# Value products of two groups and the gate product of one as seven block products, on one core

## The chip, the core and the metric

The kernel runs on one core of one Trainium2 chip. A time is the device time in microseconds of one execution on that core. Before the change the median of three executions is 239.04 us (238.83 to 239.19).

## What is computed

Attention first, then a gated feed-forward block on its output:

```python
B, H, S, D = 4, 8, 768, 64                 # q, k, v: float32 (B, H, S, D)
scores = q @ k.transpose(0, 1, 3, 2) / sqrt(D)
# heads 0, 2 and 6: causal. All others: causal, and only the first 4 keys
# and the 64 newest ones
a = softmax(where(mask, scores, -1e9))
x = (a @ v).transpose(0, 2, 1, 3).reshape(3072, 512)

gate = x @ w_gate                          # w_gate, w_val: (512, 1536)
val = x @ w_val
out = (gate * sigmoid(gate) * val) @ w_out # w_out: (1536, 512), out: float32
```

## The kernel before

**Tiles and groups.** The 3072 tokens are 24 tiles of 128, in six groups (g = 0 to 5) of four tiles, 512 tokens each. The inner dimension of 1536 is cut into 12 slices of 128 (j = 0 to 11); NJ is 12 and NK is 6. Attention is done tile by tile (tasks sc, ex, mask, val, nm: scores on TensorE, exponential on ScalarE, mask on VectorE or GpSimd, value product on TensorE, norm on VectorE). The normed tile is transposed, for 16 of the 24 tiles by a DMA that SP issues (xdma), into xt, which holds a group's x with the model dimension on partitions: 128 x 4 blocks x 512 tokens, f16.

**The feed-forward block of a group.** For each slice j: four matmuls of a 128x128 block of w_gate against 512 columns of xt, summed in one PSUM bank (task gate{g}.{j}); four for w_val into another bank (vals{g}.{j}); a tanh on ScalarE that reads the gate bank and writes sig; on VectorE the first combine, (tanh + 1) * gate, which reads sig and the gate bank and writes sil (f32, SBUF); and the second combine, 0.5 * sil * val, which reads sil and the value bank and writes slice j of h (f16, SBUF). These are the lines L759 (matmuls of both), L765, L769 and L775. Group 0 does its first slices in halves of 256 columns.

**The output product.** h (512 tokens x 1536) times w_out (1536 x 512) is done per group as a product of 2x2 blocks with seven block products instead of eight (Strassen's scheme in Winograd's form). Sums of blocks of w_out are made once (L412). Sums of blocks of h (hs{g}.{x}.{part}, x = 1 to 4 in two parts each, L831) are made by VectorE or GpSimd, 128x768 f16 with both operands in SBUF. The products out{g}.p1 to p7 (L860, 12 matmuls of 256 columns each) go into banks, and ScalarE and VectorE gather them into the output tile (oe tasks; the adds are L898), which a DMA stores (st tasks). In group 5, p2 and p3 add into banks of p1 and p5, in two parts, and come last.

**What sets the order.** All tasks are listed once, with the engines that may do each, what it depends on and which buffers it takes. Three strings of digits then settle the rest: ORDER is one global order of all tasks and some filler matmuls (each engine's program follows it), WAYS picks the engine of each task, and SLOTS the buffer or PSUM bank. The program waits for what a task depends on and for the last user of its buffer; it makes no choice at run time. The rings of buffers are these, and a gate or value bank, an attention bank or an output bank is any of eight PSUM banks of 512 f32:

```python
RINGS = {"raw": 11, "hq": 5, "e": 6, "xb": 3, "xt": 2, "sig": 2, "sil": 3,
         "ps": 8, "gv": 8, "o": 8, "big": 8}
```

h_sb holds two groups (g % 2); the second combine of group g therefore also waits for output products and sums of group g - 2 that read the same slices (`was`). Loads of the weights go through raw tiles (128 x 1024 f32) and are cast to f16. Plain copies and casts go through one function, at L206 where ScalarE does them and at L208 where VectorE or GpSimd does.

Of the kernel before, what the change touches and what calls it, by code (L numbers as in the profile page):

```python
# [7 lines left out]
FP = mybir.dt.float32  # L8
# [8 lines left out]
    "06000307090A0401081U0D1V1cy11W1X0C1d1f1e0B2021021g280g1i2229231h2B2A1j0m1r2C0h1Y1p1s2D1a0F1Z2N1q"  # L17
    "2X1b1k2E0G2O1l2W1t1m2F1u2L1x1v1w2f2M1n2g2c1y1oxk2h0n27242d25262e2l2i2m2G1z0E0y2H2I2P0z2Q2j8e2R2t"
    "8o0k8f112o2x8p8g302p108q2U312J0i132V8h2K8r2y050H8t8s8y8i8u2k983C8w8v8m323D8j2n2z3I0q8k9D8x991493"
    "3J8l9A3L8z8n94380l91903K96950o2Z9E929B3M979G2Y9F0I3N9C3U339H1C3R3V2a2q2r0j342b9h2s3S162u3O3W9c9i"  # L20
    "0r3T3X9j359d363b9I3P0J3E372v9J3Q3f3i1D2w9N9e0K1F3A9O9f3B3g2S3H9k0p179P3G0v9m9g393F9l9Q9n3h0s3Y3j"
    "9K3Z0u199r3u3a3c3n9R0x3l9s401G3k3m0w9L3o0L3d9M9S3v419o9u2T9t0M9T3p429U433w3q9v441A9p3r450R4C493e"
    "1B469q4A9X4H3y3s4B9Y9a479Z9V3t4D9b3x4Q4N4K9W4OAu9z480O4LAQ9y1H18AnA00tB2Av124RAz1EAw0P4EB0A1BE4Z"
    "B1Ap4V4Y4gB34FBH4GBF0NAxAq1Q1K4hBGAV5CArAkAWBIB41IAl0QAX1J15AY4eAy1S4IB7AZAm0SALAR3z4JAoB51MAs4d"
    "AS9wAt4f1RAM5DANB91TB69x5KBCB8BA4b5fBBAa0WBD5I4o4i4l4P4pA2A45l4m1LA34M5FAT0U1N5E4S5L1PAUAf4jA5A8"
    "1OAg4v5JAbAh4a4k4TAcAE5g4UA95n4y514q4c4zAAA60V4r0a6KACAB5o5GA7AF4WAdAD524n4sAGAiAeAK540TAj505T55"
    "4t5mAO4u5U5MAP565W4x5753AHBM4wBLBJBN5NAI5c5VAJ58595XBO4XBR5A5H5O5BBK5v5p5sBP5wBX5q5Y0YBQ600Z5r5Z"
    "5t5a0XBV5b6I5u6366BWCb6E6HBS645iCe5h6N67BY5PBTCC6O5QBbCD5R7O5d6PCM6wCc6v5xCd0cBZ68CECN71BcCF6JBa"
# [91 lines left out]
def kernel(  # L120
# [837 lines left out]
    def tasks_of_sevens(g, T_h):  # L958
# [169 lines left out]
```

## Time and profile before

| what | value |
|---|---|
| median of 3 executions | 239.04 us (238.83 to 239.19) |
| profiled execution | 239.03 us |
| its span, first to last instruction | 237.2 us |
| PE (matmuls) busy | 230.5 us, 97% |
| PEld (weight loads) busy | 146.0 us, 62% |
| DVE (VectorE) busy | 194.5 us, 82% |
| ACT (ScalarE) busy | 141.2 us, 59% |
| POOL (GpSimd) busy | 110.6 us, 47% |
| granted TensorE clock | 1.000 |
| bytes moved by DMA | 40.73 MB |

The profiled execution lies within 0.01 us of the median, so its parts may be set against the median. Busy time is a share of the span; the 1.8 us between span and execution time lie before the first and behind the last instruction. A row of a group of instructions gives line, engine, operation, what it writes and reads, its shape and type and the count, then the busy time and the mean of one in ns, then the idle time of the engine just before them and what ended it. "banks" is PSUM; every other name (raw, e, sig, sil, h_sb, hs_sb, out_sb, xt, wg_sb) is in SBUF. A row of a timeline gives the start in us from the start of the span, the length in us, and then the instruction, with the idle time before it in brackets. In the 40 slices each digit is the busy share of a slice of 5.9 us in tenths.

### The profile page before, as it was taken

What the parts mean: (1) busy time and instruction counts of PE and PEld (TensorE: products, weight loads), DVE (VectorE), ACT (ScalarE), POOL (GpSimd) and SP (SyncE); (2) the same over time, 40 slices, a digit from 0 to 9 for tenths busy, and PEclk for the clock granted to TensorE, in tenths of its full rate; (3) what the DMA queues carried; (4) which work ended last, traced back from release to release, by engine and by line L of the source; (5) the groups of instructions that cost most, each with busy time, mean ns of one, the idle gap of its engine ahead of it and who ended that gap; (6) DMA issues with size and microseconds to landing.
All of it is one profiled execution on the core that took longest, in us unless ns stands there. A gap on an engine that the chain in (4) does not pass through costs nothing.

```text
span 237.2 us, 5639 instructions
## 1 busy us (share of the span) xinstructions
PE 230.5 (97%) x2211; PEld 146.0 (62%) x2211; DVE 194.5 (82%) x362; ACT 141.2 (59%) x217; POOL 110.6 (47%) x132
## 2 busy tenths in 40 slices
PE   7899999999999999999999999999999999999994
PEld 2577865655457778655464557766555565557883
DVE  2689999998999699698968989786969867788873
ACT  3699999889599879839575485384242232231010
POOL 7386577937484940998600550884000000525500
PEclk9999999999999999999999999999999999999999
DMA  6999999999999999999798124011620000220044
GB/s 173 351 343 366 326 346 356 358 350 296 271 238 165 236 291 182 289 164 188 196 171 207 34 48 87 4 22 20 203 44 0 3 0 0 87 92 1 20 183 155
DMA packets 67194, 40.73 MB, mean 172 GB/s; under 512 B 25184, under 2 KB 61024, under 8 KB 67168
## 3 DMA queue, kind: packets, MB, share of 16 engines
q1 hardware_dynamic: 65248, 37.50, 63.4%
q10 hardware_dynamic: 1920, 2.88, 3.3%
q8 instruction: 17, 0.28, 0.5%
q14 instruction: 9, 0.07, 0.1%
HBM read 28.31 MB, written 6.29 MB: 146 GB/s over the span
## 4 chain that ended last, share of the span: by engine, by line
PE 92%; DVE 3%; DMA 2%; ACT 1%; issue 0%; DVEq 0%
PE banks L759 51%; PE banks L860 23%; PE banks L567 8%; PE banks L597 6%; PE banks L473 2%; DMA raw<-in_q_dram 2%; PE banks L621 1%; DVE wt_sb L412 1%; DVE sil L769 1%; ACT hq L206 0%; PE banks L321 0%; DVE kT L208 0%; DVE hq L212 0%; DVE qT L208 0%; DVE xb L605 0%; DVE h_sb L775 0%
## 5 line engine op out<-in xcount | busy, mean ns | idle before, releaser
L765 ACT ACTIVATE sig<-banks 128x512 f32<-128x512 f32 (+1 forms) x76 | 42.7, 574 | 54.6 <-PE banks L759 47.5
L759 PE MATMUL banks<-xt,wg_sb 128*128 128x512 f16 (+1 forms) x304 | 71.4, 368 | 0.5 <-DVE sil L769 0.5
L759 PE MATMUL banks<-xt,wv_sb 128*128 128x512 f16 (+1 forms) x304 | 70.9, 368 | 0.0
L579 ACT ACTIVATE e<-banks 128x1024 f16<-128x1024 f32 (+2 forms) x68 | 59.5, 910 | 15.0 <-PE banks L567 6.3
L769 DVE SCALAR_TENSOR_TENSOR sil<-sig,banks 128x512 f32<-128x512 f32 (+1 forms) x76 | 48.8, 655 | 14.3 <-ACT sig L765 13.6
L775 DVE SCALAR_TENSOR_TENSOR h_sb<-sil,banks 128x512 f16<-128x512 f32 (+1 forms) x76 | 48.9, 655 | 2.8 <-PE banks L759 1.8
L860 PEld LDWEIGHTS <-h_sb 128*128 128x128 f16 x420 | 40.4, 98 | 8.5
L759 PEld LDWEIGHTS <-wv_sb 128*128 128x128 f16 x304 | 28.6, 98 | 26.9
L759 PEld LDWEIGHTS <-wg_sb 128*128 128x128 f16 x304 | 28.1, 98 | 27.2 <-issue 0.8
L587 POOL TENSOR_TENSOR e<-e,m 128x640 f16<-128x640 f16 (+1 forms) x17 | 28.0, 1655 | 19.8 <-ACT e L579 19.4
L831 POOL TENSOR_TENSOR h_sb<-h_sb 128x768 f16<-128x768 f16 x13 | 21.2, 1640 | 22.5 <-DVE hs_sb L831 16.7
L898 DVE TENSOR_TENSOR out_sb<-banks,out_sb 128x512 f32<-128x512 f32 x37 | 25.1, 688 | 7.4 <-PE banks L860 7.0
L860 PE MATMUL banks<-wt_sb,h_sb 128*128 128x256 f16 x216 | 26.2, 273 | 0.0
L831 POOL TENSOR_TENSOR hs_sb<-h_sb 128x768 f16<-128x768 f16 x3 | 4.9, 1639 | 45.1 <-PE banks L860 41.2
L860 PE MATMUL banks<-wo_sb,h_sb 128*128 128x256 f16 x204 | 25.1, 273 | 0.0
L597 PEld LDWEIGHTS <-e 128*128 128x128 f16 x472 | 18.0, 97 | 5.8 <-DVE e L587 0.2
L567 PEld LDWEIGHTS <-kT 64*128 64x128 f16 x472 | 14.4, 94 | 9.3 <-issue 8.7
L567 PE MATMUL banks<-qT,kT 64*128 64x128 f16 x472 | 19.7, 218 | 0.2 <-ACT qT L206 0.2
L597 PE MATMUL banks<-vt,e 128*128 128x65 f16 x472 | 19.7, 193 | 0.1
L206 ACT CAST hq<-raw 128x1024 f16<-128x1024 f32 (+1 forms) x16 | 14.7, 936 | 5.2 <-DMA raw<-in_q_dram 3.2
L605 DVE TENSOR_TENSOR xb<-banks,rc 128x512 f16<-128x512 f32 x24 | 16.6, 692 | 0.8
L208 POOL CAST vt<-raw 64x512 f16<-64x512 f32 x23 | 14.0, 607 | 2.3 <-DMA raw<-in_v_dram 1.3
(64 smaller groups left out, 192.9 us busy)
## 6 DMA issues: line engine op xcount, KB each, us to landing
raw<-in_v_dram SPq DMA_DIRECT2D x12, 512.0 KB, 5.8
raw<-in_q_dram SPq DMA_DIRECT2D x8, 512.0 KB, 6.2
raw<-in_k_dram SPq DMA_DIRECT2D x8, 512.0 KB, 5.3
raw<-in_moe_w_gate_dram SPq DMA_DIRECT2D x6, 512.0 KB, 8.6
raw<-in_moe_w_val_dram SPq DMA_DIRECT2D x6, 512.0 KB, 8.2
raw<-in_moe_w_out_dram SPq DMA_DIRECT2D x6, 512.0 KB, 7.9
out_dram<-out_sb SPq DMA_DIRECT2D x6, 512.0 KB, 4.4
raw<-in_q_dram SPq DMA_DIRECT2D x8, 256.0 KB, 6.4
```

The costliest lines, as they stand in the source:

```text
L567: nc.tensor.matmul(sc[:, c:c + n, :], weights, moving, start=first, stop=last)
L579: nc.scalar.activation(out=to, in_=src, func=AF.Exp, scale=scale)
L587: ENG[task().way].tensor_tensor(out=ev, in0=ev, in1=mm, op=ALU.mult)
L597: nc.tensor.matmul(avs[t][:, odd, n * 66:n * 66 + 65], ee, vv, start=(m == 0), stop=(m == len(bl) - 1))
L605: nc.vector.tensor_tensor(out=xb.rearrange("p n o d -> p o n d"), in0=av[:, :, :, 0:64], in1=rc.to_broadcast([128, 2, 4, 64]), op=ALU.mult)
L759: nc.tensor.matmul(ps, wsb[:, kk, j * 128:(j + 1) * 128], xt[:, kk, c[0]:c[1]], start=(kk == 0), stop=(kk == 3))
L765: nc.scalar.activation(out=sg[g, j, c], in_=gs[g, j, c], func=AF.Tanh, scale=0.5)
L769: nc.vector.scalar_tensor_tensor(out=sl[g, j, c], in0=sg.pop((g, j, c)), scalar=1.0, op0=ALU.add, in1=gs.pop((g, j, c)), op1=ALU.mult)
L775: nc.vector.scalar_tensor_tensor(out=hs[g, j][:, c[0]:c[1]], in0=sl.pop((g, j, c)), scalar=0.5, op0=ALU.mult, in1=vs.pop((g, j, c)), op1=A ...
L831: ENG[T_hs[g, x][part].way].tensor_tensor(out=to, in0=a, in1=b, op=op)
L860: nc.tensor.matmul(rooms[g, p][:, x, lo:hi], left[:, j, 128 * x:128 * x + 128], right[:, j, lo:hi], start=(on is None and (j == 0 if apart ...
L898: nc.vector.tensor_tensor(out=cell(*to), in0=room, in1=plus, op=ALU.add)
```

## The change

The value products of groups 4 and 5 and the gate product of group 5 are done as the output product is: x (512 tokens x 512) and the weight matrix (512 x 1536) are cut into 2x2 blocks, and seven block products replace eight. Three pairs s = 0, 1, 2 each hold slices 2s and 2s+1 of the lower half of j and 6+2s and 7+2s of the upper half.

- *Sums of the weights* (vw{i}.{kk}{mat}, i = 1 to 4, two parts; L1054): 16 subtractions of 128x768 f16, ten on GpSimd and six on VectorE. Those of w_val lie in raw tiles, those of w_gate in e and hq tiles.
- *Sums of x* (xs{g}.{i}; L1084): four of 128x512 f16 for each of the two groups, five on GpSimd and three on VectorE, in a raw tile.
- *Products* (wp{g}.{s}.{p}{mat}; L1104): four matmuls of 256 columns each. Products 1, 6, 7 and 4 add up in one bank X and the bank is copied after each; product 2 has bank Y; 5 and then 3 add up in bank Z.
- *Copies* (wy; 41 on ScalarE, 4 on VectorE, through the same copy function) of a bank of 128x512 f32 into half a raw tile: r1 after product 1, u2 after 6, u3 after 7, c21 after 4, y2 after 2.
- *Adds*: c11 = r1 + y2, both in SBUF (wa, nine: eight on GpSimd, one on VectorE); c22 = u3 + Z after product 5 and c12 = u2 + Z after product 3 (wb, 18, VectorE); all L1125.
- tanh and the combines then read the cells c11, c21, c12, c22 in SBUF where they read banks before. The new forms are tanh_w, stt1_w (L1142) and stt2_w (L1148).

Of 76 gate tasks 64 are left and of 76 value tasks 52; 63 products come. Of the sums of h, VectorE does 19 instead of 31 and GpSimd 29 instead of 17. All three strings are new throughout, so the whole program is ordered anew; the filler matmuls just ahead of the first gate are five instead of nine. Lines that were there before stand three further down (L206 is L209, L759 is L762, L831 is L834, L898 is L901).

```diff
+    WINO = {"v": (4, 5), "g": (5,)}
+    HJ = DFF // 2
...
+    def msum(mat, i, kk):
...
+        if i in (1, 3):
+            a, b = MB[mat, i // 2, 1][:, kk], MB[mat, 0, i // 2][:, kk]
+        else:
+            a, b = MB[mat, 1, 1 if i == 2 else 0][:, kk], m_sums[mat, i // 2, kk]
+        ENG[T_mw[mat, i][kk].way].tensor_tensor(
+            out=m_sums[mat, i, kk], in0=a, in1=b, op=ALU.subtract)
...
+    def xsum(g, i):
...
+        a, b, op = {1: (A[1, 0], A[1, 1], ALU.add), 2: (Z[:, 0], A[0, 0], ALU.subtract),
+                    3: (A[0, 0], A[1, 0], ALU.subtract),
+                    4: (A[0, 1], Z[:, 1], ALU.subtract)}[i]
+        ENG[T_xs[g, i].way].tensor_tensor(out=Z[:, i - 1], in0=a, in1=b, op=op)
+
+    W_ON = {1: "X", 6: "X", 7: "X", 4: "X", 2: "Y", 5: "Z", 3: "Z"}
+
+    def w_product(mat, g, s, p):
+        A = x_blocks(g)
+        left = {1: A[0, 0], 2: A[0, 1], 4: A[1, 1]}.get(p)
+        if left is None:
+            left = x_sums[g][:, {5: 0, 6: 1, 7: 2, 3: 3}[p]]
...
+        begins = p in (1, 2, 5)
+        if begins:
+            w_rooms[on] = buf("gv", [128, 2, 256], FP, "gv")
+        for m in range(2):
...
+            for kk in range(2):
...
+                nc.tensor.matmul(
+                    w_rooms[on][:, m], right, left[:, kk],
+                    start=(begins and m == 0 and kk == 0), stop=(kk == 1),
+                    skip_group_check=True)
...
+    def w_copy(mat, g, s, name):
+        to = w_cell(mat, g, s, name)
+        copy(T_wc[mat, g, s, name], to, w_rooms[mat, g, s, "Y" if name == "y2" else "X"])
+
+    def w_add(mat, g, s, name):
+        to = w_cell(mat, g, s, name)
+        other = w_cell(mat, g, s, "y2") if name == "c11" else w_rooms[mat, g, s, "Z"]
+        ENG[T_wc[mat, g, s, name].way].tensor_tensor(out=to, in0=other, in1=to, op=ALU.add)
...
+    def stt1_w(g, j):
+        c = (0, 512)
+        sl[g, j, c] = buf("sil", [128, 512], FP, "sil")
+        nc.vector.scalar_tensor_tensor(
+            out=by_halves(sl[g, j, c]), in0=by_halves(sg.pop((g, j, c))), scalar=1.0,
+            op0=ALU.add, in1=w_cells("g", g, j), op1=ALU.mult)
+
+    def stt2_w(g, j):
+        hs[g, j] = h_sb[:, g % 2, j]
+        nc.vector.scalar_tensor_tensor(
+            out=by_halves(hs[g, j]), in0=by_halves(sl.pop((g, j, (0, 512)))),
+            scalar=0.5, op0=ALU.mult, in1=w_cells("v", g, j), op1=ALU.mult)
...
+            p1 = product(1, xs + w_lo)
+            r1 = copied("r1", [p1])
+            p6 = product(6, [r1, T_xs[g, 2]] + T_mw[mat, 2])
+            u2 = copied("u2", [p6])
+            p7 = product(7, [u2, T_xs[g, 3]] + T_mw[mat, 3])
+            u3 = copied("u3", [p7])
+            p4 = product(4, [u3] + T_mw[mat, 4])
+            p2 = product(2, xs + w_lo)
+            y2 = copied("y2", [p2, r1])
...
+            c11 = added("c11", [y2])
+            c21 = copied("c21", [p4, c11])
...
+            p5 = product(5, [T_xs[g, 1]] + T_mw[mat, 1])
+            c22 = added("c22", [p5, u3])
+            p3 = product(3, [c22, T_xs[g, 4]] + w_hi)
+            c12 = added("c12", [p3])
```

Two places show how the instructions stand. The first is VectorE in group 5, where its gate and value slices are combined. Before:

```order
L831 TENSOR_TENSOR h_sb<-h_sb 128x3x256
L775 SCALAR_TENSOR_TENSOR h_sb<-sil,banks 128x512
L831 TENSOR_TENSOR h_sb<-hs_sb,h_sb 128x3x256
L769 SCALAR_TENSOR_TENSOR sil<-sig,banks 128x512
L831 TENSOR_TENSOR h_sb<-hs_sb,h_sb 128x3x256
L775 SCALAR_TENSOR_TENSOR h_sb<-sil,banks 128x512 x2
L769 SCALAR_TENSOR_TENSOR sil<-sig,banks 128x512
L775 SCALAR_TENSOR_TENSOR h_sb<-sil,banks 128x512
L898 TENSOR_TENSOR out_sb<-banks,out_sb 128x2x256
```

The same stretch of VectorE's program after the change:

```order
L1142 SCALAR_TENSOR_TENSOR sil<-sig,raw 128x512
L1125 TENSOR_TENSOR raw<-banks,raw 128x512
L1142 SCALAR_TENSOR_TENSOR sil<-sig,raw 128x512 x2
L1148 SCALAR_TENSOR_TENSOR h_sb<-sil,raw 128x512 x2
L1142 SCALAR_TENSOR_TENSOR sil<-sig,raw 128x512
L1148 SCALAR_TENSOR_TENSOR h_sb<-sil,raw 128x512 x2
L1125 TENSOR_TENSOR raw<-banks,raw 128x512 x2
L1142 SCALAR_TENSOR_TENSOR sil<-sig,raw 128x512 x2
L1125 TENSOR_TENSOR raw<-banks,raw 128x512 x2
L1148 SCALAR_TENSOR_TENSOR h_sb<-sil,raw 128x512
```

The combines read a raw tile where they read a bank; adds of cells from banks stand between them, and the sums of h (L831) have left this stretch for GpSimd.

The second place is GpSimd's program from its last masks to its last sum. Before, behind the masks:

```order
L587 TENSOR_TENSOR e<-e,m_103 128x640
L587 TENSOR_TENSOR e<-e,m_102 128x1024
L831 TENSOR_TENSOR h_sb<-h_sb 128x3x256
L831 TENSOR_TENSOR hs_sb<-h_sb 128x768 x2
L831 TENSOR_TENSOR h_sb<-h_sb 128x3x256 x3
L831 TENSOR_TENSOR hs_sb<-h_sb 128x768
L831 TENSOR_TENSOR h_sb<-h_sb 128x3x256
```

After the change a part of the list reads:

```order
L1125 TENSOR_TENSOR raw<-raw 128x512
L1054 TENSOR_TENSOR e<-wg_sb 128x768
L1084 TENSOR_TENSOR raw<-xt,raw 128x512
L1054 TENSOR_TENSOR e<-wg_sb 128x768
L1054 TENSOR_TENSOR e<-wg_sb,e 128x768
L1125 TENSOR_TENSOR raw<-raw 128x512
L1084 TENSOR_TENSOR raw<-xt 128x512 x2
L1054 TENSOR_TENSOR e<-wg_sb 128x768
L1084 TENSOR_TENSOR raw<-raw,xt 128x512
L1125 TENSOR_TENSOR raw<-raw 128x512
L834 TENSOR_TENSOR h_sb<-h_sb 128x3x256
L1054 TENSOR_TENSOR hq<-wg_sb,e 128x768
```

Where eight sums of h stood behind the last masks, sums of the weights and of x, adds of cells and 17 sums of h now stand, of which this is the part ahead of group 5's.

235 lines of the change are left out of this document (180 added, 55 removed).

## The prediction

> **What bounds the kernel now.** I read the first part of the page, then the slices, the chain that ended last, and the windows of the last third.
>
> ```profile
> PE 230.5 (97%) x2211; PEld 146.0 (62%) x2211; DVE 194.5 (82%) x362; ACT 141.2 (59%) x217; POOL 110.6 (47%) x132
> ...
> PE   7899999999999999999999999999999999999994
> ...
> DVE  2689999998999699698968989786969867788873
> ...
> POOL 7386577937484940998600550884000000525500
> ...
> PE 92%; DVE 3%; DMA 2%; ACT 1%; issue 0%; DVEq 0%
> ```
>
> TensorE is the bound: busy in every slice, 92% of the chain. VectorE is the second engine; GpSimd (POOL) idles for most of the last quarter.
>
> ```profile
> 170.00:200.00 30.00, 30.00 (x199) 17.39 (x196) 23.09 (x41) 8.19 (x15) 0.00 (x0) 1.00 0.08 24
> 200.00:234.00 34.00, 33.72 (x247) 23.85 (x244) 27.51 (x47) 6.06 (x11) 11.35 (x7) 1.00 0.22 80
> ```
>
> The columns are the length, then PE, PEld, DVE, ACT and POOL busy. From 170 us on PE never stops, and POOL runs seven instructions in all. What the change spends, it spends in this stretch.
>
> The one hole in PE's work after the start is worth a look, because the change multiplies its cause:
>
> ```profile
> 59.43 1.04 POOL L208 CAST hq<-raw 128x1024 f16<-128x1024 f32 x1 [1.46 <-DMA raw<-in_q_dram]
> ...
> 59.53 1.21 DVE L412 TENSOR_TENSOR wt_sb<-wo_sb 128x512 f16<-128x512 f16 x1
> ...
> 61.73 1.46 PE L759 MATMUL banks<-xt,wg_sb 128*128 128x512 f16 x6 [0.50 <-DVE sil L769]
> ...
> L412 DVE TENSOR_TENSOR wt_sb<-wo_sb x3: 411/414/1212, 59.5 to 62.8; 128x512 f16<-128x512 f16 x3
> ...
> L831 DVE TENSOR_TENSOR h_sb<-h_sb x9: 548/552/559, 87.7 to 220.6; 128x768 f16<-128x768 f16 x9
> L587 DVE TENSOR_TENSOR e<-e,m x21: 483/683/693, 23.7 to 169.0; 128x1024 f16<-128x1024 f16 x14, 128x640 f16<-128x640 f16 x7
> ...
> L769 DVE SCALAR_TENSOR_TENSOR sil<-sig,banks x76: 413/682/690, 21.0 to 218.4; 128x512 f32<-128x512 f32 x68, 128x256 f32<-128x256 f32 x8
> ...
> 39.34 0.69 DVE L587 TENSOR_TENSOR e<-e,m 128x1024 f16<-128x1024 f16 x1
> ...
> 39.76 1.16 POOL L208 CAST wg_sb<-raw 128x1024 f16<-128x1024 f32 x1 [1.18 <-DMA raw<-in_moe_w_gate_dram]
> ```
>
> A DVE subtraction with both operands in SBUF started 0.10 us behind a POOL cast and took 1.21 us; its like take 0.41. It ended 0.27 us after the cast did (60.74 against 60.47): it stood until POOL was through, and DVE, then PE (0.50 us), stood with it. In the other order POOL's cast at 39.76, begun under a two-operand DVE mask, took 1.16 us against 1.04. So a DVE instruction that reads two operands from SBUF and a POOL instruction exclude each other. It is rare here: the longest of the L831 and L587 groups is within 10 ns of the usual. The combines of L769 and L775 read one operand from PSUM, and their longest is 690 ns although POOL works 47% of the span.
>
> **The change, part by part.** Times below count from T, the start of the first new product on PE (wp4.0.1v: group 4, pair 0, product 1, value matrix); a place T+x on PE is the sum of PE's tasks up to there in the new order.
>
> *PE.* 36 tasks of four 512-column matmuls go, 63 products of four 256-column ones come.
>
> ```profile
> 111.35 6.91 PE banks L759 x32
> ...
> 220.62 13.11 PE banks L860 x120
> ...
> 232.24 1.47 PE L860 MATMUL banks<-wo_sb,raw 128*128 128x256 f16 x12
> ```
>
> 6.91/32 = 0.216 us and 13.11/120 = 0.1093 us. Gone: 144 x 0.216 = 31.1. Added: 252 x 0.1093 = 27.5. PE saves 3.6 us. The profiled execution took 239.03 us (span 237.2; the median of the runs is 239.04), so with PE as dense as before: 235.5. From T PE then has 12 gate tasks (10.4), 63 products (27.5), 22 output products (28.8), two scores and two value steps (about 1.5): 68.2 us. The last matmul ended at 233.71 (232.24 + 1.47); 3.6 earlier and 68.2 back puts T at 161.9. Products 1, 6, 7 and 4 pile up in one bank with a copy between them, nine times; PE's order puts other tasks between (3.9 us from product 6 to 7 of the first pair). Without that cover each of 27 copies would cost some 0.6 us, 16 in all.
>
> *ACT.* 41 copies of 512 from PSUM.
>
> ```profile
> L206 ACT COPY out_sb<-banks 128x512 f32<-128x512 f32 x3 | 1.7, 582 | 0.0
> ```
>
> 41 x 0.58 = 24 us, in an engine that is busy for 14 of the 64 us above: hidden.
>
> *DVE.* 18 adds and 4 copies from PSUM, one add of two SBUF tiles, three sums of x, six of weights; 12 sums of h leave for POOL.
>
> ```profile
> 183.62 1.28 DVE L769 SCALAR_TENSOR_TENSOR sil<-sig,banks 128x512 f32<-128x512 f32 x2
> ...
> 169.95 1.02 DVE L831 TENSOR_TENSOR hs_sb<-h_sb 128x768 f16<-128x768 f16 x2
> ...
> L898 DVE TENSOR_TENSOR out_sb<-banks,out_sb 128x512 f32<-128x512 f32 x37 | 25.1, 688 | 7.4 <-PE banks L860 7.0
> ```
>
> Back to back, one follows the other after 0.60 us (1.28 - 0.68) or 0.47 (1.02 - 0.55). From the first wb4 (T+9.1, behind wp4.1.2v) to the last combine of group 5 stand 80 instructions: 78 x 0.60 + 2 x 0.47 = 47.7, done at T+56.8. Output product 5 of group 5 starts at T+60.4 on a dense PE and needs one POOL sum (1.6) behind that combine. Taken alone, DVE just keeps up.
>
> *What the combines read.* The cells of the new products lie in SBUF. The 24 last combines of groups 4 and 5 and the 12 first ones of group 5 now read two SBUF operands (L1148, L1142): 36 instructions of the kind that stood at 59.53. An f32 SCALAR_TENSOR_TENSOR on two SBUF operands has no row. Below: it runs beside POOL like the PSUM one, no price; above: it waits for POOL like the f16 subtraction. I take the second, since what the blocked row has and the never-blocked L769 row lacks is the second SBUF operand.
>
> The Trainium skill, page "SBUF — State Buffer", section "Who interferes with whom", says the same in general: a DVE instruction with two SBUF inputs and a GpSimd instruction that reads SBUF exclude each other, and the later one waits for the whole of the earlier. The rows at 59.43 and 39.34 agree. By that rule the sum is the 254 below; by what the rows show for f16 alone it is the 240.9 of the first rival.
>
> *POOL.* At the same time POOL's list becomes long.
>
> ```profile
> 204.24 3.24 POOL L831 TENSOR_TENSOR hs_sb<-h_sb 128x768 f16<-128x768 f16 x2 [41.25 <-PE banks L860]
> 207.44 1.64 POOL L831 TENSOR_TENSOR h_sb<-h_sb 128x768 f16<-128x768 f16 x1
> ...
> 74.20 1.16 POOL L412 TENSOR_TENSOR wt_sb<-wo_sb,wt_sb 128x512 f16<-128x512 f16 x1 [3.64 <-DVE wt_sb L412]
> 75.31 1.16 POOL L412 TENSOR_TENSOR wt_sb<-wo_sb 128x512 f16<-128x512 f16 x1
> 76.42 2.14 POOL L587 TENSOR_TENSOR e<-e,m 128x1024 f16<-128x1024 f16 x1
> ```
>
> So 1.60 us each for 768 elements, 1.11 for 512. From its first add of cells (wa4.0.c11v) to the last sum that output product 7 of group 5 needs (hs5.3.1) POOL has 21 of the first kind (16 sums of h, 5 of weights) and 13 of the second (8 adds, 5 sums of x): 33.6 + 14.4 = 48.0. The f32 adds have no row; 1.11, the same count in f16, is the lower end; the upper is 2.1, as many bytes as the last row's mask, and would add 8 us. I take the lower, whose row is an add of two tensors of the same count too.
>
> *The sum.* Two-operand DVE instructions in that stretch, up to the last combine: 36 combines and one add at 0.60, six f16 sums at 0.47: 25.0. If they and POOL exclude each other, 48.0 + 25.0 = 73.0 us stand in one line. Some of each start-up lies under the other's work: the cast at 39.76 lost 0.12 us to a mask that ran on for 0.27, so 0.15 were hidden; the blocked subtraction needed 0.27 after its release instead of 0.41, so 0.14. With that off each duration (POOL 1.49 and 1.01, DVE 0.54 and 0.41) it is 44.4 + 22.4 = 66.8. The line starts when ACT has copied product 2 of the first pair:
>
> ```profile
> 10.78 4.83 ACT L579 ACTIVATE e<-banks 128x1024 f16<-128x1024 f32 x5
> ...
> L206 ACT COPY vt<-vt x12: 448/462/466, 38.4 to 142.5; 2x330 f16<-2x330 f16 x12
> ```
>
> Behind product 1 (0.44) ACT has three copies of 0.58, two exponentials of 0.95 and two small copies of 0.46: T+5.0. So the line ends at T+71.8 to T+78.0, where a dense PE wants it at T+61.7 (product 7). From there PE has 6.55 us left, and 5.3 follow the last matmul (239.03 - 233.71): 161.9 + 71.8 + 6.55 + 5.3 = 245.6, to 251.8. The line also has holes, while POOL waits for DVE and DVE does PSUM work: four PSUM instructions ahead of the last combine of group 4 (hs4.1.1 waits for it) and four ahead of that of group 5: 8 x 0.60 = 4.8. So 250.4 to 256.6; I take the middle, **254**. At worst all 23 PSUM instructions that stand behind the tenth combine of group 4 are holes, 13.8 instead of 4.8, which gives 266; the early sums of POOL, which wait for nothing on DVE, argue for the smaller number.
>
> *Replanned rest.*
>
> ```profile
> 5.19 1.14 ACT L206 CAST hq<-raw 128x512 f16<-128x512 f32 x2 [3.18 <-DMA raw<-in_q_dram]
> ...
> 5.30 0.99 POOL L267 MEMSET nat<- 32x128 f16 x4
> 8.40 0.61 POOL L208 CAST hq<-raw 128x512 f16<-128x512 f32 x1 [2.11 <-PE banks L473]
> 8.95 0.31 POOL L313 MEMSET vt<- 128x96 f16 x2
> ```
>
> The first query cast goes half to POOL, behind the mask work and the memset at 8.95: done at 6.29 + 0.31 + 0.61 = 7.2 instead of 6.3. In return nine filler matmuls (0.22 each) between there and the first gate become five, and that gate waits for the gate weights, whose place in the load queue is unchanged. I take 0, with 0.5 either way. Weight sums and late loads fall into slices where POOL has room. On SP four transposes bring group 5's x:
>
> ```profile
> L615 SPq DMA_TRANSPOSE xt<-xb x16: 1189/1231/2592, 65.4 to 173.7; - x16
> ...
> DMA to landing us min/median/max: 2.4/2.9/5.3
> ```
>
> The last two wait for the norm of tile 23 (T+8.2 on a dense PE), land about T+12.5 (1.2 + 1.2 + 1.9 later at most) and are wanted at T+15.0. If that norm is late, their delay lies inside the line above.
>
> **Rivals.** *Only f16 pays.*
>
> ```profile
> 58.68 0.21 DVE L604 RECIPROCAL rc<-banks 128x8 f32<-128x8 f32 x1
> 58.92 0.69 DVE L605 TENSOR_TENSOR xb<-banks,rc 128x512 f16<-128x512 f32 x1
> ```
>
> These two are a norm, 0.85 us back to back (0.24 + 0.61). The combines run freely and only the f16 sums wait. Between T+5.0 and the norm of tile 23 DVE has four of them against four POOL instructions: 5.0 + 1.11 + 1.60 + 1.11 + 1.60 + 4 x 0.47 + 0.85 ends at T+13.2. The gate task gate4.1.0 takes the bank which that norm frees and stands at T+8.5: 4.7 us of PE lost. Later vw4.1g stands behind vw4.0g, up to 1.5. That is 240.2 to 241.7, say 240.9. For it: the only blocked row is f16. Against: nothing in that row hangs on the type.
>
> *The gain arrives* (the other side). DVE and POOL pass each other, or POOL runs its early sums ahead; then PE is dense but for about 0.6 us at product 5 and 7 of group 5: 236.1. It decides if the four sums ahead of that norm wait under 3.6 us in all. For it: DVE alone ends at T+56.8, in time, PE's cut is certain, and the f32 form has no row that shows it waiting. Against it: the row at 59.53.
>
> *PE waits for copies.* If the cover of the piled products goes too, up to 16 us come on top of 235.5: 251. Against it: ACT is busy for 14 of the last 64 us. Its time lies with the forecast's, so it has no chance of its own.
>
> **How the numbers follow.** Forecast 0.70, its own range 246 to 264: one fully blocked row is the whole evidence, so no more. Only f16 pays: 0.13. Gain: 0.13. About as before, the waits just eating 3.6 us: 0.04. Less than 0.2% cannot be told from no change here, so faster 0.13, same 0.04, slower 0.83. The range of 240 to 264 takes in the first rival and leaves out the gain, the case of no change and the tail towards 266: about 0.2.
>
> **What would show it.** Right: combines of L1142 and L1148 with durations spread from 0.68 to over 2 us while `banks` adds of L1125 stay at 0.69; PE idle after T, released by DVE and POOL; POOL almost gapless after 170 us; L1104 matmuls at 0.109 us. Wrong: flat combines and a dense PE (the gain), or flat combines with one PE hole of some 5 us ahead of gate4.1.0 (the first rival). If PE's granted clock fell in the holes, the time would go above 264.

## The result and the profile after

The changed kernel takes 258.79 us (258.67 to 259.55, four executions) where the kernel before takes 239.0: 1.083 times the time, interval 1.081 to 1.086. The forecast was 254, range 240 to 264. The profiled execution took 258.73 us with a span of 256.9. Three of the runs below (the 14 sums with the combines, and silu with 16 and with eight sums on DVE) had one execution each in a slower state of the chip, and their medians leave it out.

The page of the changed kernel, busy times and then slices for PE, DVE, POOL and the granted clock:

```profile
PE 233.0 (91%) x2319; PEld 158.0 (61%) x2319; DVE 224.1 (87%) x373; ACT 169.0 (66%) x277; POOL 171.4 (67%) x157
...
PE   7799999999999999999999999969958987738993
...
DVE  1879999799997987998678789999999999999974
...
POOL 7594789659769039995097736494989478881620
PEclk9999999999999999999999999999997999985999
```

Until slice 26 PE is as full as before. Then it has gaps, DVE is full in every slice but the last two, and POOL, which did almost nothing in these slices before, works through them. What PE waited for, in us in all, times, longest:

```profile
PE banks L1104 <- DVE raw L1125: 7.8, 3, 5.1
PE banks L1104 <- ACT raw L209: 4.7, 3, 2.1
PE banks L762 <- DVE xb L608: 1.9, 1, 1.9
...
PE banks L863 <- DVE out_sb L901: 1.1, 2, 0.9
PE banks L762 <- DVE sil L772: 0.8, 1, 0.8
PE banks L863 <- DVE raw L889: 0.7, 1, 0.7
```

That is 17.0 us of holes where there were none behind 162 us. PE's busy time rose by 2.5 us (233.0 against 230.5) although its work shrank, because part of it ran at half clock (below). 17.0 + 2.5 = 19.5, and the last matmul ended 19.6 us later (253.35, the start 251.88 and 1.47, against 233.71). So the loss is PE waiting, and DVE is what it waited for; ACT's copies, named in the second row, themselves waited for DVE to free their raw tiles (4.9 us for L1148, 4.1 us for L1142).

What DVE was doing shows in its groups, here with minimum, median and maximum of one in ns:

```profile
L1148 DVE SCALAR_TENSOR_TENSOR h_sb<-sil,raw x24: 675/893/2124, 177.1 to 241.9; 128x512 f16<-128x512 f32 x24
...
L1142 DVE SCALAR_TENSOR_TENSOR sil<-sig,raw x12: 674/707/2128, 201.6 to 236.6; 128x512 f32<-128x512 f32 x12
...
L1125 DVE TENSOR_TENSOR raw<-banks,raw 128x512 f32<-128x512 f32 x18 | 11.8, 677 | 0.0
L778 DVE SCALAR_TENSOR_TENSOR h_sb<-sil,banks 128x512 f16<-128x512 f32 x44 | 29.6, 683 | 4.0 <-PE banks L762 3.0
```

The same instruction takes 683 ns where one operand is in PSUM and anything from 675 to 2128 where both are in SBUF. The longest hole of PE shows how it comes about. First DVE, then POOL, then PE:

```profile
225.44 1.75 DVE L1142 SCALAR_TENSOR_TENSOR sil<-sig,raw 128x512 f32<-128x512 f32 x1
227.11 4.16 DVE L1148 SCALAR_TENSOR_TENSOR h_sb<-sil,raw 128x512 f16<-128x512 f32 x2
231.20 1.28 DVE L1125 TENSOR_TENSOR raw<-banks,raw 128x512 f32<-128x512 f32 x2
```

```profile
225.03 1.61 POOL L1125 TENSOR_TENSOR raw<-raw 128x512 f32<-128x512 f32 x1 [0.67 <-ACT raw L209]
226.96 3.77 POOL L834 TENSOR_TENSOR h_sb<-h_sb 128x768 f16<-128x768 f16 x2 [0.31 <-PE banks L863]
```

```profile
225.33 1.47 PE L863 MATMUL banks<-wo_sb,h_sb 128*128 128x256 f16 x12
231.93 1.01 PE L1104 MATMUL banks<-raw,wg_sb 128*128 128x256 f16 x4 [5.12 <-DVE raw L1125]
```

Two combines need 4.16 us instead of 1.28, because each stands behind a sum of POOL; POOL's two sums need 3.77 us, since the second stands behind a combine. The add from PSUM that PE waits for (c22, ahead of product 3) stands behind both combines in DVE's queue, and PE waits 5.12 us for it.

### The profile page after: what moved, and what is told of

It reads as the page before. It is cut to its first block, busy times and chain, and to the rows that moved or that the text cites. A ratio compares the mean times of both kernels' runs of the same rounds, so it can differ in the third digit from the quotient of the medians.

```text
span 256.9 us, 5991 instructions
## 1 busy us (share of the span) xinstructions
PE 233.0 (91%) x2319; PEld 158.0 (61%) x2319; DVE 224.1 (87%) x373; ACT 169.0 (66%) x277; POOL 171.4 (67%) x157
## 3 DMA queue, kind: packets, MB, share of 16 engines
q10 hardware_dynamic: 2192, 3.41, 3.7%
## 5 line engine op out<-in xcount | busy, mean ns | idle before, releaser
L762 PE MATMUL banks<-xt,wg_sb 128*128 128x512 f16 (+1 forms) x256 | 59.7, 366 | 2.7 <-DVE xb L608 1.9
L762 PE MATMUL banks<-xt,wv_sb 128*128 128x512 f16 (+1 forms) x208 | 47.8, 363 | 0.0
L772 DVE SCALAR_TENSOR_TENSOR sil<-sig,banks 128x512 f32<-128x512 f32 (+1 forms) x64 | 40.5, 648 | 4.9 <-ACT sig L768 3.2
L762 PEld LDWEIGHTS <-wg_sb 128*128 128x128 f16 x256 | 24.0, 98 | 24.4 <-issue 3.1
L778 DVE SCALAR_TENSOR_TENSOR h_sb<-sil,banks 128x512 f16<-128x512 f32 (+1 forms) x52 | 32.7, 642 | 4.0 <-PE banks L762 3.0
L209 ACT COPY raw<-banks 128x512 f32<-128x512 f32 x41 | 22.7, 592 | 18.8 <-PE banks L1104 9.7
L834 POOL TENSOR_TENSOR h_sb<-h_sb 128x768 f16<-128x768 f16 x17 | 29.8, 1761 | 7.7 <-DVE hs_sb L834 7.2
L1148 DVE SCALAR_TENSOR_TENSOR h_sb<-sil,raw 128x512 f16<-128x512 f32 x24 | 30.7, 1304 | 0.5 <-ACT raw L209 0.5
L762 PEld LDWEIGHTS <-wv_sb 128*128 128x128 f16 x208 | 19.0, 98 | 17.2
L901 DVE TENSOR_TENSOR out_sb<-banks,out_sb 128x512 f32<-128x512 f32 x37 | 24.8, 683 | 4.8 <-PE banks L863 3.9
L1125 POOL TENSOR_TENSOR raw<-raw 128x512 f32<-128x512 f32 x8 | 12.8, 1600 | 13.5 <-ACT raw L209 9.9
L834 POOL TENSOR_TENSOR hs_sb<-h_sb 128x768 f16<-128x768 f16 x7 | 12.2, 1749 | 12.6 <-DVE sil L1142 5.9
L600 PE MATMUL banks<-vt,e 128*128 128x65 f16 x472 | 19.6, 193 | 0.0
```

Source lines behind the costliest of these rows:

```text
L600: nc.tensor.matmul(avs[t][:, odd, n * 66:n * 66 + 65], ee, vv, start=(m == 0), stop=(m == len(bl) - 1))
L762: nc.tensor.matmul(ps, wsb[:, kk, j * 128:(j + 1) * 128], xt[:, kk, c[0]:c[1]], start=(kk == 0), stop=(kk == 3))
L772: nc.vector.scalar_tensor_tensor(out=sl[g, j, c], in0=sg.pop((g, j, c)), scalar=1.0, op0=ALU.add, in1=gs.pop((g, j, c)), op1=ALU.mult)
L778: nc.vector.scalar_tensor_tensor(out=hs[g, j][:, c[0]:c[1]], in0=sl.pop((g, j, c)), scalar=0.5, op0=ALU.mult, in1=vs.pop((g, j, c)), op1=A ...
L834: ENG[T_hs[g, x][part].way].tensor_tensor(out=to, in0=a, in1=b, op=op)
L901: nc.vector.tensor_tensor(out=cell(*to), in0=room, in1=plus, op=ALU.add)
```

## The experiments

All times are medians; each ratio is against the kernel before on the same chip.

| run | us | ratio (interval) |
|---|---|---|
| before, combines of two groups on two SBUF operands | 245.79 | 1.027 (1.023 to 1.031) |
| before, 20 more GpSimd sums | 272.12 | 1.137 (1.135 to 1.139) |
| both | 279.69 | 1.170 (1.167 to 1.172) |
| before, 14 more GpSimd sums, placed later | 244.27 | 1.021 (1.020 to 1.023) |
| those 14 and the combines | 258.73 | 1.084 (1.081 to 1.087) |
| changed kernel, combines on one SBUF operand | 238.32 | 0.997 (0.995 to 0.998) |
| changed kernel, 16 sums of h on DVE | 252.41 | 1.056 (1.054 to 1.057) |
| changed kernel, filler matmuls in two holes | 257.57 | 1.077 (1.076 to 1.079) |
| silu on ScalarE, 16 sums on DVE | 245.44 | 1.026 (1.023 to 1.028) |
| silu on ScalarE, eight sums on DVE | 247.66 | 1.035 (1.033 to 1.037) |
| silu on ScalarE, GpSimd empty | 243.43 | 1.016 (1.013 to 1.019) |
| silu into PSUM, GpSimd as in the change | 240.21 | 1.004 (1.003 to 1.005) |

### One SBUF operand instead of two, in the changed kernel

```diff
-        nc.vector.scalar_tensor_tensor(
-            out=by_halves(sl[g, j, c]), in0=by_halves(sg.pop((g, j, c))), scalar=1.0,
-            op0=ALU.add, in1=w_cells("g", g, j), op1=ALU.mult)
+        nc.vector.tensor_reduce(out=by_halves(sl[g, j, c]), in_=by_halves(sg.pop((g, j, c))).unsqueeze(3),
+                                axis=mybir.AxisListType.X, op=ALU.max)
...
-        nc.vector.scalar_tensor_tensor(
-            out=by_halves(hs[g, j]), in0=by_halves(sl.pop((g, j, (0, 512)))),
-            scalar=0.5, op0=ALU.mult, in1=w_cells("v", g, j), op1=ALU.mult)
+        nc.vector.tensor_reduce(out=by_halves(hs[g, j]), in_=w_cells("v", g, j).unsqueeze(3),
+                                axis=mybir.AxisListType.X, op=ALU.max)
```

> The changed kernel, in which the 36 combines that read cells become an instruction of the same count on one SBUF operand (a maximum over an axis of one: the first reads sig, the second the value cell; the product of the two is left out, so the output is not the reference's). Everything else stays: products, copies, adds, all sums of GpSimd, the order. Theory (two SBUF operands against GpSimd): these 36 stay at one length, 0.6 to 0.7 us, PE's holes after 170 us shrink to those of the f16 sums, and the time falls to the first rival's sum of the prediction, 241, within 238 to 245. Rival (the holes come from the chain product, copy, product or from DVE's number of instructions): 251 to 259.

Measured: 238.32 us, 20.5 us less than the change: the whole loss of 19.8 and a little more. The two instructions that replace the combines, by group, and the one hole of PE of a microsecond or more behind 10 us:

```profile
L1147 DVE TENSOR_REDUCE h_sb<-raw 128x512 f16<-128x512 f32 x24 | 15.6, 678 | 0.4 <-POOL h_sb L834 0.4
L1142 DVE TENSOR_REDUCE sil<-sig 128x512 f32<-128x512 f32 x12 | 7.8, 678 | 0.0
...
172.28 1.02 PE L762 MATMUL banks<-xt,wg_sb 128*128 128x512 f16 x4 [1.93 <-DVE xb L608]
```

GpSimd's list, the products, their copies and their chain, the number of DVE instructions and the order are those of the change. So none of them is what costs the time: it is the second SBUF operand. (The instruction is another one here; the next pair of runs changes the operand alone.) The hole that is left stands where the rival "only f16 pays" put it, ahead of the task gate4.1.0. PE's busy time is 227.6 us here, 2.9 less than before: the saving on PE is real.

### The two halves of the collision, in the kernel before

The kernel before has neither products nor copies. It was given the two sides of the collision apart: combines of groups 4 and 5 that read two SBUF operands (sig or sil a second time; the gate and value banks are left out), and sums on GpSimd that nobody needs.

```diff
-            in1=gs.pop((g, j, c)), op1=ALU.mult)
+            in1=sg_again if g >= 4 else gs.pop((g, j, c)), op1=ALU.mult)
...
-            in1=vs.pop((g, j, c)), op1=ALU.mult)
+            in1=sl_again if g >= 4 else vs.pop((g, j, c)), op1=ALU.mult)
```

```diff
             P.tasks[number].run()
+            if P.tasks[number].name == "hs2.4.1":
+                flat = wo_sb.rearrange("p a b -> p (a b)")
+                for _ in range(14):
+                    nc.gpsimd.tensor_tensor(out=spare, in0=flat[:, 0:768],
+                                            in1=flat[:, 768:1536], op=ALU.subtract)
```

The sums shown are the 14 of the second pair of runs; in the first pair 20 of them stood behind `mask22.0`.

> The kernel before, in which all combines of groups 4 and 5 read two SBUF operands (the first one sig twice, the second one sil twice; the gate and value banks are left out of the product, so the output is not the reference's). GpSimd does nothing from 170 to 204 us there. Theory (a DVE instruction with two SBUF operands waits only for a running GpSimd instruction): combines stay near 0.68 us until GpSimd's sums from 204 us on, time 239.0, at most 1 us more. Rival (such a combine is dearer by itself): every one of the 48 longer, and the time up by 2 us or more.

Measured: 245.79, more than expected. Of the 48 combines 41 ran without a GpSimd instruction beside them and took 676 to 694 ns, so the form is not dearer by itself. The other seven met the few sums that GpSimd has in this kernel from 204 us on, and five of them took 1.6 to 2.1 us. A stretch of the timeline:

```profile
204.95 3.69 POOL L833 TENSOR_TENSOR hs_sb<-h_sb 128x768 f16<-128x768 f16 x2 [41.24 <-PE banks L862]
...
205.51 3.67 DVE L777 SCALAR_TENSOR_TENSOR h_sb<-sil 128x512 f16<-128x512 f32 x2
...
208.60 2.08 POOL L833 TENSOR_TENSOR h_sb<-h_sb 128x768 f16<-128x768 f16 x1
209.11 2.11 DVE L770 SCALAR_TENSOR_TENSOR sil<-sig 128x512 f32<-128x512 f32 x1
...
211.87 0.38 PE L759 MATMUL banks<-xt,wg_sb 128*128 128x512 f16 x1 [3.56 <-DVE out_sb L900]
```

Three combines take 5.8 us, and PE stands for 3.56 us. Five sums of GpSimd were enough for 6.7 us; the expectation was wrong in taking them for harmless. Part of the 6.7 is PE's clock, halved behind that hole from 213.15 to 216.57 us: the one execution at full clock took 244.43.

> The kernel before with 20 more GpSimd subtractions of 128x768 f16 (wo_sb into a tile that nobody reads) behind its mask at about 170 us, 32 us of work; the combines read PSUM as before. Theory: the combines of L769 and L775 do not wait, only DVE's f16 sums do, some ten of them by up to 1.6 us each: 239 to 242. Rival (a long list on GpSimd slows DVE whatever it reads): combines between 172 and 204 us longer than 0.69 us, time above 245.

> Both at once: combines of groups 4 and 5 on two SBUF operands, and the 20 GpSimd subtractions. Theory: some 30 combines (0.59 each) and seven f16 sums (0.5) share one line with 20 sums of 1.53: 52 us where 32 were, so GpSimd ends near 225 us instead of 204 and DVE, which had some 7 us of slack in 30, falls back by 10 to 15 us: 246 to 256, with single combines at about 2.1 us. Rival (no exclusion for the f32 combine): as the run with the GpSimd sums alone, 239 to 242.

Measured: 272.12 and 279.69. These two say nothing on the theory, and both missed what was expected. The 20 sums were put ahead of a sum of group 2 on GpSimd, and an output product needed that one:

```profile
PE banks L861 <- POOL h_sb L832: 31.6, 1, 31.6
```

PE stood 31.6 us for a badly placed list. The pair was repeated with 14 sums behind that one:

> The kernel before with 14 more GpSimd subtractions of 128x768 f16 (wo_sb into a tile that nobody reads), now behind the sum hs2.4.1, so that no sum which the output needs stands behind them until 204 us: 22 us of work in GpSimd's idle stretch. Combines read PSUM as before. Theory (only DVE instructions with two SBUF operands wait): combines stay at 0.68 us, some eight f16 sums of DVE wait up to 1.6 us each, time 239 to 241. Rival (a busy GpSimd slows every DVE instruction): combines between 172 and 195 us above 0.75 us and a time above 243.

Measured: 244.27. The combines, on PSUM, did not feel the busy GpSimd; the f16 sums of DVE, on two SBUF operands, did. Minimum, median and maximum of the combines, and a stretch of DVE and of GpSimd:

```profile
L776 DVE SCALAR_TENSOR_TENSOR h_sb<-sil,banks x76: 406/681/690, 22.9 to 226.9; 128x512 f16<-128x512 f32 x68, 128x256 f16<-128x256 f32 x8
```

```profile
184.28 0.68 DVE L770 SCALAR_TENSOR_TENSOR sil<-sig,banks 128x512 f32<-128x512 f32 x1
185.06 0.69 DVE L776 SCALAR_TENSOR_TENSOR h_sb<-sil,banks 128x512 f16<-128x512 f32 x1
185.67 0.68 DVE L208 COPY out_sb<-banks 128x512 f32<-128x512 f32 x1
186.27 1.13 DVE L832 TENSOR_TENSOR h_sb<-hs_sb,h_sb 128x768 f16<-128x768 f16 x1
187.32 1.99 DVE L832 TENSOR_TENSOR h_sb<-h_sb 128x768 f16<-128x768 f16 x1
189.23 0.67 DVE L776 SCALAR_TENSOR_TENSOR h_sb<-sil,banks 128x512 f16<-128x512 f32 x1
```

```profile
179.98 8.91 POOL L1095 TENSOR_TENSOR spare<-wo_sb 128x768 f16<-128x768 f16 x5
```

Beside the same five GpSimd sums the three instructions that read a bank take 0.68 to 0.69 us and the two sums that read SBUF twice take 1.13 and 1.99 instead of 0.55. The mechanism is as expected; the time, 5.2 us, is over the expected 0 to 2, because the delayed sums put combines off that PE waits for, for their banks or for h (four PE holes, 4.3 us).

> The same 14 subtractions, and all combines of groups 4 and 5 on two SBUF operands as in the run with those alone (245.8 us). Theory: 14 x 1.53 = 21.4 us of GpSimd stand in one line with some 20 combines (0.59) and five f16 sums (0.5) of that stretch; DVE, which was busy for 77% of it, can hide some 5 us of the 21, so 10 to 16 us come on top: 254 to 262. Rival (what cost 6.7 us there was something else than GpSimd's sums): 245 to 248.

Measured: 258.73, within the expected range. Alone the combines cost 6.7 us and the sums 5.2, together 19.6, far more than the 11.9 of both: each side costs little where the other has little to do. In the trace PE's holes behind 162 us add up to 15.0 us, against 4.7 and 4.3 with one side alone. Half clock behind them takes its part of the time too: 13.7 us of this trace ran at it, 3.4 of that with the combines alone and none with the sums alone.

### GpSimd's sums of h moved to DVE

```diff
             t.way = t.ways[int(w)]
+            if t.name.startswith(('hs4', 'hs5')):
+                t.way = "DVE"
```

> The changed kernel with the 16 sums of h of groups 4 and 5 moved from GpSimd to VectorE, at the same places of the global order. Theory (the line that GpSimd and DVE's two-operand instructions share sets the end): 16 x 1.53 = 24.5 us leave that line and 16 x 0.5 = 8 come to it, so it ends some 16 us earlier; what is then late is DVE's own list, near T+65 where PE wants T+62: 240 to 246. Rival (DVE's list is what is too long): 8 us more on DVE, 264 to 268.

Measured: 252.41, a gain of 6.4 us where 13 to 19 were expected. The direction is that of the theory (the rival had 264 and more), but the size was wrong. The windows say why; the columns are length, PE, PEld, DVE, ACT and POOL busy:

```profile
212.00:222.00 10.00, 8.03 (x71) 6.75 (x70) 10.00 (x17) 7.05 (x14) 1.27 (x1) 1.00 0.28 107
222.00:232.00 10.00, 8.26 (x75) 7.10 (x74) 10.00 (x17) 4.75 (x10) 1.84 (x1) 1.00 0.00 0
232.00:242.00 10.00, 7.51 (x66) 6.28 (x65) 10.00 (x19) 0.00 (x0) 0.00 (x0) 1.00 0.27 103
```

GpSimd is almost out of it and DVE is full: what was then late was DVE's own list. In the change the line that both engines share was too long; with the 16 sums on it, DVE's list alone is.

### The clock behind the holes

In ORDER one entry of eight filler matmuls into bank 5 (3788, written z6) stands ahead of product 4 of the last gate pair, and two of eleven into bank 4 (3775, yt) ahead of product 3:

```diff
-    "HHIbIIIfHII0GOHoIcHJHPIJHsI4INHKGNI5I1IKHOI8I2HQGPIRI6I9IOISHRGIGSIPIAI3HSGZI7IBGRIgITIjGTIhIkIo"
...
+    "HHIbIIIfHII0GOHoIcHJHPIJHsI4INz6HKGNI5I1IKHOI8I2HQGPIRI6I9IOISytytHRGIGSIPIAI3HSGZI7IBGRIgITIjGT"
```

> The changed kernel with 30 filler matmuls (0.216 us each, into banks that are free) where PE stands longest: 22 ahead of the product that waited 5.1 us at 226.5 to 231.9 us, eight ahead of that which waited 1.9 us at 222 us. They keep PE busy in holes and compute nothing. Theory of the size (PE's granted clock fell to 0.5 behind the long hole, from 231.9 to about 236.8, and the line of GpSimd and DVE then waited for PE's slow products): the clock stays at 1.0 there, PE gains 2.4 us and the line about 1.5: 256 to 258. Rival (GpSimd's line sets the end whatever PE's clock does): 258.8, within 0.5.

Measured: 257.57, within the expected range: 1.2 us less than the change, although the filler computes nothing. Windows of the changed kernel, then of this one (the last three columns are granted clock, DMA share and GB/s):

```profile
227.00:232.00 5.00, 0.07 (x1) 0.07 (x1) 5.00 (x5) 1.62 (x3) 3.73 (x2) 0.77 0.00 0
232.00:237.00 5.00, 5.00 (x27) 3.52 (x27) 4.51 (x8) 1.63 (x3) 0.35 (x1) 0.55 0.00 0
```

```profile
227.00:232.00 5.00, 4.62 (x23) 2.06 (x22) 5.00 (x5) 1.62 (x3) 3.68 (x2) 1.00 0.00 0
232.00:237.00 5.00, 5.00 (x46) 4.33 (x45) 5.00 (x7) 1.74 (x3) 2.34 (x2) 1.00 0.00 0
```

PE got through 46 matmuls instead of 27 in the same 5 us. Product 3 starts at 231.93 us in the changed kernel and at 231.88 here, so the two are level up to there, and 1.2 of the 19.8 us come from the clock and not from the waits themselves.

### Versions that keep the products without the collision

Four versions tried to keep PE's saving. All let ScalarE apply silu in one step in groups 4 and 5, which takes 24 first combines off DVE. The first three also add c11 from the bank on DVE (no copy y2, no GpSimd add) and move sums to DVE:

```diff
+            nc.scalar.activation(out=sl[g, j, c], in_=gs.pop((g, j, c)), func=AF.Silu)
...
+        nc.scalar.activation(out=by_halves(sl[g, j, c]), in_=w_cells("g", g, j), func=AF.Silu)
...
+        if name == "y2":
+            to = w_cell(mat, g, s, "c11")
+            nc.vector.tensor_tensor(out=to, in0=w_rooms[mat, g, s, "Y"], in1=to, op=ALU.add)
+            return
```

> A version meant to keep PE's 3.6 us without the collisions. The changed kernel with four edits: in groups 4 and 5 ScalarE applies silu in one step to the gate bank or cell (no tanh, no first combine: 24 DVE instructions of 0.60 us less, 12 of them with two SBUF operands); c11 = r1 + product 2 is added by DVE straight from the bank in place of the copy y2 (nine copies of ScalarE and eight GpSimd adds less); the 16 sums of h of groups 4 and 5 go to DVE; the sum hs3.3.0 stands behind the norm of tile 23, which the first hole of 1.9 us waited for. Theory (the shared line and a full DVE were the whole loss): GpSimd has 13 sums left behind 162 us (some 19 us) and DVE some 8 instructions less than the changed kernel's 80 with its 16 sums added; PE is dense again and the time is 236 to 239, that is faster than before by up to 1.2%. Rival (24 combines on two SBUF operands still stand in line with the weight sums of group 5, and DVE, full in every window after 172 us, stays late): 241 to 248.

> The same, but only the sums of h of group 5 move to DVE; those of group 4 stay on GpSimd, where they stand in line with the combines of group 5. Theory of the line: eight sums of 1.53 on GpSimd against eight of 0.5 on DVE, some 4 to 8 us of DVE waiting in the stretch 205 to 225 us: slower than the version with all 16 on DVE by 0 to 5 us. Rival (DVE's number of instructions decides): faster than that version by up to 3 us.

Measured: 245.44 with 16 sums on DVE, 247.66 with eight. The order of the two is the one that the line of both engines gives (each sum that stays on GpSimd costs the line more than on DVE), but neither came near 239: both lie in the range of the rival, in which DVE stays late.

> The version with silu on ScalarE and c11 added from the bank, and now every sum that GpSimd did behind 164 us on DVE (16 sums of h of groups 4 and 5, four of group 3, five weight sums, five sums of x), some of them moved behind the norm of tile 23; two copies of DVE go to ScalarE. GpSimd does nothing from about 166 us on, so no DVE instruction can wait for it. Reason: a sum of 128x768 on GpSimd beside a DVE that always has a two-operand instruction next costs that line 1.53 us, on DVE 0.47. In the version with eight sums left on GpSimd DVE was busy for 69 of 80 us behind 162 us, with some 14 us of waiting in it; the sums add 21 x 0.45 = 9.5 us of work and take away the 14. Theory: PE dense but for about 2 us, 236 to 239.5. Rival (products and copies, not the two engines, leave PE's holes): 242 to 246.

Measured: 243.43. The combines on two SBUF operands ran at 684 ns with nothing beside them, as they should, and PE still had holes:

```profile
L1154 DVE SCALAR_TENSOR_TENSOR h_sb<-sil,raw 128x512 f16<-128x512 f32 x24 | 16.1, 684 | 0.9 <-ACT raw L209 0.9
```

```profile
PE banks L1109 <- DVE raw L1136: 2.4, 2, 2.0
...
PE banks L868 <- DVE raw L1127: 1.1, 2, 0.9
PE banks L868 <- DVE raw L894: 1.0, 1, 1.0
PE banks L1109 <- ACT raw L209: 0.7, 1, 0.7
```

Emptying GpSimd brings 15.4 of the 19.8 us back and has a price of its own. In the longest hole, which ended at 180.59 us, five sums of weights stood in DVE's queue shortly ahead of the add that PE waited for, in an order that was made for other work; behind it the clock was halved for 3.4 us. DVE was not full (busy for 52.1 of the 60 us from 172 to 232). The time lies in the rival's range, 242 to 246; what makes up the other holes was not taken apart.

The last version leaves GpSimd its whole list and takes the second SBUF operand away instead: ScalarE writes silu into PSUM, in place into the gate bank in group 4 and into two spare banks in group 5 (20 of 24 second combines; four found no bank).

```diff
+            if j > 0:
+                sl[g, j, c] = gs[g, j, c]
+            nc.scalar.activation(out=sl[g, j, c], in_=gs.pop((g, j, c)), func=AF.Silu)
...
+    SPARE_BANKS = {6: 4, 3: 4, 9: 5, 8: 5, 2: 5, 5: 4, 4: 5, 10: 4, 11: 4}
...
+            sl[g, j, c] = banks[:, 512 * n:512 * n + 512]
```

> The changed kernel with its long GpSimd list left as it is, but with the second combines of groups 4 and 5 reading one SBUF operand: ScalarE applies silu in one step (no tanh, no first combine, as before in the versions with silu) and writes it into PSUM, for group 4 in place into the gate bank, for group 5 into two banks that are free late; the second combine then reads silu from the bank and the value cell from SBUF. Four of 24 still read it from SBUF for want of a bank. Some second combines stand earlier, so that a gate bank comes free in time, and the sums hs3.3.0 and vw2.1g stand behind the norm of tile 23. Theory (two SBUF operands beside GpSimd were the whole loss): combines at 0.68 us beside a GpSimd that works on; 24 DVE instructions less than in the run with one-operand combines, which took 238.3 with one hole of 1.9 us that the moved sums close: 236 to 238.5, faster than before by 0.3 to 1.2%. Rival (it is the chain of products, copies and buffers that was late in the versions with silu, and PSUM banks held longer make it later): 241 to 246.

Measured: 240.21, against an expected 236 to 238.5. The combines, by group, and what PE still waited for behind 162 us:

```profile
L1155 DVE SCALAR_TENSOR_TENSOR h_sb<-banks,raw 128x512 f16<-128x512 f32 x20 | 13.6, 688 | 11.3 <-ACT banks L777 6.4 <-ACT raw L209 2.9 <-ACT banks L1151 1.9
```

```profile
PE banks L762 <- DVE raw L211: 1.1, 1, 1.1
PE banks L870 <- DVE h_sb L1155: 1.0, 1, 1.0
PE banks L870 <- DVE raw L1132: 0.5, 1, 0.5
PE banks L1111 <- DVE h_sb L1155: 0.5, 1, 0.5
...
PE banks L870 <- DVE raw L896: 0.3, 1, 0.3
```

18.6 of the 19.8 us come back with GpSimd as busy as in the change (164.5 us of 238.4). The 24 first combines that silu takes off DVE help here too, so this run does not show what the operand alone is worth; the run with one operand does. The 3.4 us that PE still waits are new ones: banks are held until the second combine, and DVE now idles ahead of combines that wait for ScalarE. None of the versions beats the kernel before; whether another order of the last one would (240.2 - 3.4 is 236.8) was not tried.

## Why the prediction was right, by its own steps

- *PE is the bound and the change saves it 3.6 us.* Right, and nearly in size: 2.9 us less busy time where PE is dense (the run with one SBUF operand). The first new product started at 161.51; T was put at 161.9.
- *ACT's copies and the piled products are covered.* Right: with one-operand combines no hole of PE behind 162 us is released by ACT. The rival "PE waits for copies" would have left that run at 251.
- *DVE taken alone just keeps up.* Right, with little to spare: with one operand it is busy for 57.5 of the 60 us from 172 to 232, and PE is dense. Eight microseconds more of work (the 16 sums) were too much.
- *Two SBUF operands on DVE and a GpSimd instruction exclude each other, in f32 too.* Right, and shown from both sides: beside GpSimd's sums the same combine takes up to 2.12 us on two SBUF operands and at most 0.69 on one. The Trainium skill, page "SBUF — State Buffer", section "Who interferes with whom", states this rule and also that a DVE instruction with at most one SBUF input stays free of GpSimd outside some faster modes; the runs here agree with both halves (676 to 694 ns alone; 671 to 687 ns for the one-operand instructions in the place of the combines).
- *The line of both engines.* It was to hold 66.8 to 73.0 us of work and 4.8 us of holes from T+5.0. It ran from 166.72 us to the end of hs5.3.1 at 246.04, 79.3 us: 71.2 of work and 8.2 of holes. The work came out as worked out: one sum of 768 added 1.53 us to the line (1.49 assumed), an add of cells 1.16 (1.01 to 1.11), a combine 0.59 (0.54), each counted from the end of the instruction before it in the line. The holes are the term that was too small, by 3.4 us. They were counted as eight PSUM instructions of DVE; the trace has more of these in them (1.1 us each at 175.95, 210.94 and 231.28), and once DVE itself stood 0.5 us, at 235.36, for a copy of ACT that came late behind a product at half clock.
- *From there to the end 6.55 and 5.3 us.* PE's product 7 of group 5 started at 245.72, 0.32 us ahead of the end of that sum, which only its second half needs; one more hole of 0.7 us followed (L889, c22 late on DVE). 253.35 + 5.4 = 258.7.
- *254 against 258.8.* 3.4 us are the holes of the line and 1.3 its work, above the middle of the range that was taken. 1.2 us of this go back to the clock, which the prediction had named only as a way past 264; it fell twice, and the time stayed below that.
- *The rivals.* "Only f16 pays" became a run of its own, and its price was too high: 238.3, not 240.9. Four f16 sums of DVE were to wait ahead of the norm of tile 23; two did (0.5 and 1.4 us), and PE lost 1.9 us instead of 4.7. "The gain arrives" has the right size for what it supposes: 238.3 - 1.9 = 236.4 against 236.1.
- *What would show it.* The spread of L1142 and L1148 and the flat L1125 came as written. "POOL almost gapless" was wrong: it is the line of both engines that is nearly gapless (8.2 of 79.3 us); POOL alone is busy for 61.6 of the 97 us behind 160.

## What to carry to other kernels

Before an operand moves from PSUM to SBUF, count the SBUF operands that each DVE instruction then reads, and what GpSimd does at that time: two long lists that each fit can be one list that does not. Moving GpSimd's work to DVE cures that only where DVE has room; taking one operand back to PSUM, with the first combines gone to ScalarE, cured nearly all of it here. And when freed work on the bound engine is paid for with work on the second engine, look at what is left of the second one: here DVE had little to spare, and PE's 2.9 us never arrived.

## What was not expected of the hardware

The granted clock does not follow the length of a hole alone. In the changed kernel matmuls of 256 columns ran at 0.213 us instead of 0.109 for 3.4 us behind a hole of 2.13 us (ended at 192.12); in the run with filler a hole of the same length at the same place (ended at 192.07) was followed by matmuls at 0.109, and so it was in the run with the sums on DVE. In the hole of 5.12 us the clock fell at 229.69 and came back at 236.52. The Trainium skill, page "TensorE: Matmul & The Clock Gate", section "Part 1: The HAM clock gate", puts the fall to half clock behind an idle window of about 3.4 us of a free-running count; that a hole's place against such a count matters fits the pair of 2.13 us, but a fall behind 2.13 us is sooner than an idle window of 3.4 us would give.

The granted clock in the traces settles it. Every change lies on a grid of 3.41 us that runs on from the first rise. In the changed kernel the window from 188.73 to 192.15 us held the whole hole of 2.13 us, and the clock fell at its end; in the run with filler a window ended at 191.47, inside the hole, and split it into 1.53 and 0.60. Over 13 traces (all but that of silu with 16 sums on DVE) all 23 windows at full clock with 2.01 us or more without a matmul ended in half clock, and none of the 879 others did, the emptiest of which had 1.94. So a window need not be idle throughout: some six tenths of it were enough here. Full clock came back only behind a window without a hole. Between 1.94 and 2.01 us, and for windows at half clock with holes under 2.2 us, nothing is shown.
